# Chunked attention into a two-layer MLP: w_in and w_out loads in halves, the first layer of block 0 in 128-token pieces, s3 on VectorE in the last blocks

## The chip, the cores and the metric

The kernel runs on one core of one Trainium2 chip. The metric is device time in microseconds (us) from one execution; lower is better. A core has five engines that run side by side and wait for each other through semaphores: TensorE (PE in the profile; its weight loads are PEld), VectorE (DVE), ScalarE (ACT), GpSimd (POOL) and SyncE (SP). Work on an engine runs in the order in which it was issued. TensorE writes to PSUM, which has eight banks of 128 x 512 float32; everything else lives in SBUF.

## The reference

```python
# q, k, v: [8 batches, 8 heads, 576, 64], in chunks of 64 tokens, 9 chunks a batch
scores = q_c @ k_c.T / sqrt(64)              # within a chunk only
attn   = softmax(scores)
x      = (attn @ v_c) -> [4608 tokens, 512]  # heads side by side
h      = x @ w_in                            # 512 -> 2048
g      = h * sigmoid(beta * h)
out    = g @ w_out                           # 2048 -> 512
```

Inputs and output are float32; the kernel computes its products in float16 with float32 sums.

## The kernel before

The 4608 tokens are nine blocks j of 512 tokens. For each block there is attention (scores, exponential, product with v, division by the sum), then the first layer L1(j), then the second layer L2(j). The order on every engine is written out by hand: `tc.manual_schedule()` keeps the order of the Python calls, and hooks place pieces of one stage between the matmuls of another. Attention of block j + 1 is placed inside L2(j).

The names that matter here:

- `load_qk`, `load_v`, `load_w_in`, `load_w_out` issue loads on POOL's DMA queue, which convert float32 to float16. w_in comes in four column pieces of 512, w_out in four pieces of four 128-row groups (`kk`, 0 to 15). POOL's transfers use eight completion semaphores in turn.
- `emit_T(b, z, which)` transposes q or k of batch b on VectorE (line 136), one half z at a time.
- `emit_sc(g)` makes scores of four chunks on TensorE (line 168) and their exponentials on ScalarE (line 177). `emit_pv(i, where)` multiplies 128 tokens with v (line 198) and divides on VectorE (lines 210 to 215). `emit_xp(i)` transposes those 128 tokens on TensorE (line 232) and copies them into `xt` (line 235). Blocks 0 and 1 use `emit_xp`; later blocks use a transposing DMA on SP's queue.
- `emit_h(j, m)` is the matmul of L1 for hidden group m (128 of the 2048 hidden columns, line 258); `emit_g(j, m)` is its Silu on ScalarE (line 268). `emit_m` is both. `L1_plain` runs 16 groups in this way for blocks 0 and 1.
- `L2_plain(j)`, block 0 only, is 16 units (four w_out pieces times four 128-token groups), line 510; each token group's last unit copies its bank out, on ScalarE or VectorE in turn (lines 525 and 527), and stores it.
- Blocks 1 to 8 use Strassen-like sums: L2 (`steps_L2`, steps `mm[0]` to `mm[6]`, line 411) needs the sums s1 to s4 of g (`emit_sum`, lines 369 to 375) and t1 to t4 of w_out (`emit_tw`, line 383); from block 2 on L1 (function `L1`) needs sums of x and of w_in (`emit_sw`, lines 280 to 283).
- `scale_w_out` multiplies w_out groups by 1/beta (VectorE line 127, ScalarE line 123), because Silu is applied to beta * h.
- `emit_idle` issues matmuls of zeros; their results aren't used.
- `table(func)` makes ScalarE load the table of a function (line 582).

PSUM is held in three pools: `ps_p` has four one-bank buffers handed out in turn, `ps_s` has two banks (tags sc0 and sc1), and `ps_x` has one buffer of two banks (tag x). A new tile in a buffer waits until the old one has been read. In the last blocks `fill` is a list of sums, which `dve(n)` takes from its head.

s3 is made in four parts. Before the change two of them run on POOL in every block:

```python
tt = (nc.gpsimd if which == 3 and part in (0, 2) else nc.vector).tensor_tensor
```

Of the kernel before, what the change touches and what calls it, by code (L numbers as in the profile page):

```python
# [15 lines left out]
def kernel(  # L16
# [85 lines left out]
                    in_=v[b, h0:h0 + 2].rearrange("s (c p) d -> p (s c) d", p=CH),  # L102
                )

    def load_w_in(g):
        n = DFF // 4
        nc.gpsimd.dma_start(
            out=w_in16[g],
            in_=moe_w_in[:, g * n:(g + 1) * n].rearrange("(k p) f -> p k f", p=128),
        )  # L110

    def load_w_out(g):
        n = NM // 4
        nc.gpsimd.dma_start(
            out=w_out16[:, g * n:(g + 1) * n].rearrange("p m r d -> p m (r d)"),
            in_=moe_w_out[g * n * 256:(g + 1) * n * 256, :].rearrange(
                "(m p r) d -> p m (r d)", p=128, r=2),
        )

    def scale_w_out(g, act=0):  # L120
        for n, kk in enumerate(range(4 * g, 4 * g + 4)):
            if n < act:
                nc.scalar.activation(
                    out=wo(kk), in_=wo(kk), func=ACTF.Copy,
                    scale=binv[:, kk % 2, kk // 2:kk // 2 + 1])
                continue
            nc.vector.tensor_scalar_mul(wo(kk), wo(kk), binv[:, kk % 2, kk // 2:kk // 2 + 1])
# [96 lines left out]
        else:  # L224
            x16_t[i] = xf

    def emit_xp(i):
        xf = x16_t.pop(i)
        j, t0 = i // 4, (i % 4) * 128
        xps = ps_s.tile([128, KDM, 128], FP16, tag=f"sc{i % 2}", name="xps")  # L230
        for kk in range(KDM):
            nc.tensor.transpose(
                out=xps[:, kk, :], in_=xf[:, kk * 128:(kk + 1) * 128], identity=ident
            )
        nc.scalar.copy(out=xt_t[j][:, :, t0:t0 + 128], in_=xps)  # L235

    def emit_idle(n, w=512, d=None):
        if d is None:
# [9 lines left out]
    hps_t = {}  # L248
    w_r = [t.rearrange("p k (m i r) -> p k m r i", r=2, i=128) for t in w_in16]

    def emit_h(j, m, c0=0, c1=BLK):
        if m == 0 and c0 == 0 and j == 0:
            gt_t[j] = gt_p.tile([128, KFF, BLK], FP16, tag="gt", name="gt")
        if c0 == 0:
            hps_t[j, m] = ps_p.tile([128, BLK], FP32, tag="p", name="hps")
        for n in range(KDM):
            e, z = n // 2, n % 2
            nc.tensor.matmul(  # L258
                out=hps_t[j, m][:, c0:c1],
                lhsT=w_r[m // 4][:, 2 * z + e, m // 2 % 2, m % 2, :],  # L260
                rhs=xt_t[j][:, n, c0:c1],
                start=(n == 0),
                stop=(n == KDM - 1),
            )

    def emit_g(j, m):
        hps = hps_t.pop((j, m))
        nc.scalar.activation(  # L268
            out=gt_t[j][:, m, :], in_=hps, func=ACTF.Silu,
            scale=beta2[:, m % 2, m // 2:m // 2 + 1],  # L270
        )
# [89 lines left out]
    def emit_sum(j, which, part):  # L361
        if j not in s_t:
            s_t[j] = [s_p.tile([128, NM, HT], FP16, tag=f"s{i}", name=f"s{i}") for i in range(4)]
        s1, s2, s3, s4 = s_t[j]
        g = gt_t[j]
        lo, hi = slice(2 * part, 2 * part + 2), slice(NM + 2 * part, NM + 2 * part + 2)
        tt = (nc.gpsimd if which == 3 and part in (0, 2) else nc.vector).tensor_tensor
        if which == 1:
            tt(out=s1[:, lo], in0=g[:, lo, dn], in1=g[:, hi, dn], op=ALU.add)  # L369
        elif which == 2:  # L370
            tt(out=s2[:, lo], in0=s1[:, lo], in1=g[:, lo, up], op=ALU.subtract)  # L371
        elif which == 3:
            tt(out=s3[:, lo], in0=g[:, lo, up], in1=g[:, lo, dn], op=ALU.subtract)  # L373
        else:
            tt(out=s4[:, lo], in0=g[:, hi, up], in1=s2[:, lo], op=ALU.subtract)
# [130 lines left out]
    def L2_plain(j):  # L506
        ops = [ps_p.tile([128, DM], FP32, tag="p", name="ops") for _ in range(4)]

        def part(kk, t):
            nc.tensor.matmul(  # L510
                out=ops[t],
                lhsT=gt_t[j][:, kk, t * 128:(t + 1) * 128],
                rhs=wo(kk),
                start=(kk == 0),
                stop=(kk == KFF - 1),
            )

        def unit(g, t):
            for kk in range(4 * g, 4 * g + 4):
                part(kk, t)  # L520
            if g < 3:
                return
            osb = osb_p.tile([128, DM], FP32, tag="osb", name="osb")
            if t % 2:
                nc.vector.tensor_copy(out=osb, in_=ops[t])
            else:
                nc.scalar.copy(out=osb, in_=ops[t])
            r0 = j * BLK + t * 128
            nc.sync.dma_start(out=out[r0:r0 + 128, :], in_=osb)

        return [lambda g=g, t=t: unit(g, t) for g in range(4) for t in range(4)]

    fill = []

# [2 lines left out]
            if fill:  # L537
                fill.pop(0)()

    def L1_plain(j, hooks, nh):  # L540
        if j:
            gt_t[j] = gt_p.tile([128, KFF, BLK], FP16, tag="gt", name="gt")
        for m in range(nh):
            emit_h(j, m, 0, HT)
            hooks.get(-1 - m, lambda: None)()
        for m in range(nh):
            emit_h(j, m, HT, BLK)
            emit_g(j, m)
        for m in range(nh, KFF):
            hooks.get(m, lambda: None)()  # L550
            emit_m(j, m)
            if j and m == 8:
                for p in (0, 2):
                    emit_sum(j, 3, p)
        if j:
            for p in range(4):
                fill.extend([lambda w=w, p=p: emit_sum(j, w, p) for w in (1, 2)])
            hooks.get(KFF, lambda: None)()

    def L1(j, hooks={}, first=None):  # L560
        gt_t[j] = gt_p.tile([128, KFF, BLK], FP16, tag="gt", name="gt")

        def sp(m):
            def f():
                hooks.get(m, lambda: None)()
                emit_m(j, m)
            return f

        if first:
            first()  # L570
        unit(j, 0, [sp(8), sp(9), sp(10)])
        unit(j, 1, [sp(11), sp(12), sp(13)])
        for p in (0, 2):
            emit_sum(j, 3, p)
        for p in (0, 2, 1, 3):
            fill.extend([lambda w=w, p=p: emit_sum(j, w, p) for w in (1, 2)])
        sp(14)()
        sp(15)()
        hooks.get(KFF, lambda: None)()

    def table(func):
        nc.scalar.activation(out=warm2, in_=warm, func=func, scale=1.0)  # L582

    with tc.manual_schedule():
# [11 lines left out]
            nc.vector.memset(t[:, :, :, D:D + 1], 1.0)  # L596
        load_v(0)
        make_identity(nc, ident)
        for g in range(4):
            load_w_in(g)  # L600
        load_w_out(0)
        load_w_out(1)
        load_qk(1)
        load_w_out(2)
        load_v(1)
        load_w_out(3)
        load_qk(2)

        emit_idle(4)
        for f in T_items(0):  # L610
# [13 lines left out]
        emit_sc(1, where="p")  # L624
        emit_idle(3)
        emit_pv(0, xbar=False)
        emit_pv(1, where="p", xbar=False)
        d = emit_idle(4, 256)
        emit_xp(0)
        emit_pv(2, xbar=False)  # L630
        emit_idle(2, d=d)
        emit_xp(1)
        emit_pv(3, where="p", xbar=False)
        emit_idle(3, d=d)

        L1_plain(0, {-2: lambda: emit_xp(2), -3: lambda: emit_xp(3)}, 4)
        emit_sw()
        scale_w_out(0)
        scale_w_out(1)
        emit_tw(1)  # L640
        T1 = T_items(1)
        T1[0]()
        T1[1]()
        T1[2]()
        T1[3]()
        scale_w_out(2, act=2)
        table(ACTF.Exp)
        load_v(2)
        load_qk(3)
        hooks = {  # L650
            8: lambda: [emit_sc(2, "x"), emit_sc(3)],
            10: lambda: [emit_pv(4, xbar=False), emit_pv(5, "s", xbar=False), scale_w_out(3, act=2)],
            12: lambda: [emit_pv(6, xbar=False), emit_xp(4), emit_xp(5)],
            14: lambda: [emit_pv(7, xbar=False), emit_xp(6)],
        }
        for kk, f in enumerate(L2_plain(0)):
            hooks.get(kk, lambda: None)()
# [17 lines left out]
        for j in range(1, NB):  # L675
            na = j + 1
            late = j == 1
            if late:
                L1_plain(1, {
                    -1: lambda: [emit_xp(7), table(ACTF.Silu)], 3: lambda: emit_tw(3), 4: lambda: T(2), 5: lambda: T(2),  # L680
                    6: lambda: emit_tw(2), 7: lambda: T(2), 9: lambda: T(2),
                    10: lambda: emit_tw(4), 14: lambda: T(3), 15: lambda: T(3),
                    11: lambda: [loads(1), loads_v(1)],
                    KFF: lambda: [table(ACTF.Exp), emit_sc(4, "x"), emit_sc(5)],
                }, 3)
            else:
                L1(j, {8: lambda: loads(j), 10: lambda: T(j + 2), 11: lambda: loads_v(j),
                       13: lambda: T(j + 2), 14: lambda: T(j + 2) if j + 2 < B else dve(2),
                       15: lambda: dve(2) if j + 2 >= B else None})

            def pv(n, where):
                if na < NB:
# [80 lines left out]
```

## Time and profile before

| what | value |
|---|---|
| median of 8 runs | 278.48 us (277.59 to 280.51) |
| the profiled execution, its time | 279.58 us |
| its span, first to last instruction | 277.8 us |
| TensorE busy | 263.4 us, 95% of the span |
| VectorE busy | 218.2 us, 79% |
| ScalarE busy | 163.5 us, 59% |
| POOL busy | 102.4 us, 37% |
| first matmul of L1(0), first of L2(0), first of L1(1) | 18.42, 33.37, 50.43 us |
| granted TensorE clock | full over the whole span |

The page lists one execution: busy time of each engine, the span in 40 slices, DMA queues, the chain that ended last, and groups of instructions by line. A row of the timeline gives the start in us, the duration in us, the engine, the line, the operation, what it writes and reads, the shape and how many instructions the row merges; a note in brackets gives how long the engine had been idle and what released it. Waits of an engine are inferred from semaphore events. A time "from start to start" between two instructions of one engine is often shorter than their durations, since they are pipelined.

### The profile page before, as it was taken

The page shows a single profiled execution, that of the slowest core. Times are in us where ns is not written, and L with a number is a line of the kernel's source. Part 1 is how long each engine was busy: PE and PEld are TensorE (multiplying, and loading weights), DVE is VectorE, ACT ScalarE, POOL GpSimd, SP SyncE. Part 2 cuts the span into 40 slices and gives each one's busy share as a digit, 9 for nine tenths or more (in the row PEclk, how much of TensorE's full clock was granted, in tenths as well). Part 3 has the DMA queues.
Part 4 walks back from the last instruction along what each step waited for, and adds up shares of the span by engine and source line. Part 5 has one row for each costly group of instructions (what it writes and reads, how often), then busy time and mean ns, then how long its engine had stood idle before and what let it go on. Part 6 is the DMA issues. An engine that isn't in the chain of part 4 may idle for free.

```text
span 277.8 us, 8206 instructions
## 1 busy us (share of the span) xinstructions
PE 263.4 (95%) x3513; PEld 188.5 (68%) x3513; DVE 218.2 (79%) x425; ACT 163.5 (59%) x276; POOL 102.4 (37%) x108
## 2 busy tenths in 40 slices
PE   2689999999999999999999999999999999999995
PEld 0355454647776688668866886688767866787684
DVE  2772655879588998899889988997689768996874
ACT  2149746788066845783578457845783478216820
POOL 8742252190108720862087205620351035013500
PEclk9999999999999999999999999999999999999999
DMA  6999999999877924892389243924202320232013
GB/s 102 173 207 211 211 182 208 217 238 187 67 134 144 168 46 115 163 166 50 112 155 171 45 117 82 80 46 114 76 2 57 99 76 0 57 100 76 2 38 114
DMA packets 69588, 31.99 MB, mean 115 GB/s; under 512 B 53680, under 2 KB 63920, under 8 KB 69552
## 3 DMA queue, kind: packets, MB, share of 16 engines
q0 software_dynamic: 44960, 18.35, 54.8%
q1 hardware_dynamic: 24448, 12.99, 17.7%
q8 instruction: 27, 0.44, 0.6%
q10 hardware_dynamic: 144, 0.13, 0.1%
q14 instruction: 9, 0.07, 0.1%
HBM read 36.71 MB, written 9.44 MB: 166 GB/s over the span
## 4 chain that ended last, share of the span: by engine, by line
PE 75%; DVE 13%; DMA 6%; issue 2%; POOL 2%; ACT 1%; DVEq 0%; ACTq 0%; POOLq 0%
PE hps L258 24%; PE oA L411 15%; PE wA L311 8%; PE wX L311 6%; PE ops L510 5%; PE oD L411 5%; PE oC L411 3%; PE oB L411 3%; DMA vb<-in_v_dram 3%; DMA xt<-x 3%; DVE x L215 3%; DVE s L369 2%; DVE s L371 2%; PE scx L168 1%; PE sc L168 1%
## 5 line engine op out<-in xcount | busy, mean ns | idle before, releaser
L258 PE MATMUL hps<-xt,wi 128*128 128x512 f16 (+1 forms) x380 | 85.2, 363 | 0.3 <-ACT xt L235 0.2
L268 ACT ACTIVATE gt<-hps,beta 128x512 f16<-128x512 f32 x88 | 57.4, 681 | 20.4 <-PE hps L258 20.3
L258 PEld LDWEIGHTS <-wi 128*128 128x128 f16 x380 | 37.0, 98 | 29.0 <-issue 0.7
L411 PEld LDWEIGHTS <-s 128*128 128x128 f16 x496 | 47.4, 98 | 7.0 <-issue 0.7
L411 PE MATMUL oA<-tw,s 128*128 128x256 f16 x368 | 44.4, 273 | 0.4 <-issue 0.4
L411 PEld LDWEIGHTS <-gt 128*128 128x128 f16 x384 | 36.2, 98 | 6.6
L422 ACT COPY u<-oA 128x512 f32<-128x512 f32 x24 | 14.0, 585 | 44.2 <-PE oA L411 44.2
L99 POOL DMA_DIRECT2D vb<-in_v_dram x32 | 27.4, 874 | 9.2 <-DMA wi<-in_moe_w_in_dram 5.4
L319 DVE COPY u<-wA 128x512 f32<-128x512 f32 x42 | 28.6, 681 | 2.5 <-PE wA L311 2.5
L342 POOL TENSOR_TENSOR t<-u,w 128x512 f32<-128x512 f32 x14 | 17.8, 1273 | 33.1 <-DVE u L319 33.1
L311 PEld LDWEIGHTS <-sw 128*128 128x128 f16 x224 | 21.9, 98 | 9.5 <-issue 1.0
L480 POOL TENSOR_TENSOR o<-t,o 128x512 f32<-128x512 f32 x7 | 8.9, 1271 | 52.4 <-ACT o L477 43.6
L449 POOL TENSOR_TENSOR w<-u,u 128x512 f32<-128x512 f32 x7 | 9.8, 1407 | 44.2 <-ACT u L422 22.8
L136 DVE STREAM_TRANSPOSE qT<-qu 128x576 f32<-128x576 f32 x16 | 20.0, 1251 | 5.0 <-DMA qu<-in_q_dram 5.0
L373 POOL TENSOR_TENSOR s<-gt 128x512 f16<-128x512 f16 x16 | 20.3, 1285 | 9.5 <-ACT gt L268 9.5
L136 DVE STREAM_TRANSPOSE kT<-ku 128x576 f32<-128x576 f32 x16 | 19.9, 1245 | 3.9 <-DMA ku<-in_k_dram 3.9
L369 DVE TENSOR_TENSOR s<-gt 128x512 f16<-128x512 f16 x32 | 20.6, 645 | 0.0
L311 PEld LDWEIGHTS <-wi 128*128 128x128 f16 x168 | 16.4, 98 | 4.9
L371 DVE TENSOR_TENSOR s<-s,gt 128x512 f16<-128x512 f16 x32 | 18.1, 567 | 1.1
L322 ACT ACTIVATE gt<-c,beta 128x512 f16<-128x512 f32 x28 | 18.6, 715 | 0.3
L168 PEld LDWEIGHTS <-kT 32*64 32x64 f16 x1152 | 11.3, 106 | 10.3 <-DVE kT L136 6.5
L582 ACT ACT_TABLE_LOAD x14 | 18.0, 1283 | 0.2
(87 smaller groups left out, 402.6 us busy)
## 6 DMA issues: line engine op xcount, KB each, us to landing
out_dram<-osb SPq DMA_DIRECT2D x21, 256.0 KB, 3.0
vb<-in_v_dram POOLq DMA_DIRECT2D x32, 144.0 KB, 7.8
qu<-in_q_dram POOLq DMA_DIRECT2D x7, 576.0 KB, 7.5
ku<-in_k_dram POOLq DMA_DIRECT2D x7, 576.0 KB, 9.6
out_dram<-o SPq DMA_DIRECT2D x14, 256.0 KB, 2.2
wi<-in_moe_w_in_dram POOLq DMA_DIRECT2D x4, 512.0 KB, 11.9
w_out<-in_moe_w_out_dram POOLq DMA_DIRECT2D x4, 512.0 KB, 16.2
qu<-in_q_dram POOLq DMA_DIRECT2D x2, 288.0 KB, 5.5
```

Of the source, the lines that this page charges most:

```text
L99: nc.gpsimd.dma_start(out=t[64 * hp:64 * hp + 64, 2 * z:2 * z + 2, :, 0:D].rearrange("p s c d -> p (s c) d"), in_=v[b, h0:h0 + 2].rearrang ...
L136: nc.vector.transpose(out=dst[b][:, z].rearrange("p t r e -> p (t r e)").bitcast(FP32).rearrange("p (t r) -> p r t", r=RUN), in_=src[b][:, ...
L258: nc.tensor.matmul(out=hps_t[j, m][:, c0:c1], lhsT=w_r[m // 4][:, 2 * z + e, m // 2 % 2, m % 2, :], rhs=xt_t[j][:, n, c0:c1], start=(n == ...
L268: nc.scalar.activation(out=gt_t[j][:, m, :], in_=hps, func=ACTF.Silu, scale=beta2[:, m % 2, m // 2:m // 2 + 1],)
L311: nc.tensor.matmul(out=bank[b][:, i, :], lhsT=a[:, kk, q, i, :], rhs=rhs[:, kk, :], start=(first and i == 0 and kk == 0), stop=(kk == 1), ...
L319: nc.vector.tensor_copy(out=sb[nm], in_=bank[b])
L322: nc.scalar.activation(out=gt_t[j][:, m, cols], in_=src, func=ACTF.Silu, scale=beta2[:, m % 2, m // 2:m // 2 + 1],)
L369: tt(out=s1[:, lo], in0=g[:, lo, dn], in1=g[:, hi, dn], op=ALU.add)
L371: tt(out=s2[:, lo], in0=s1[:, lo], in1=g[:, lo, up], op=ALU.subtract)
L373: tt(out=s3[:, lo], in0=g[:, lo, up], in1=g[:, lo, dn], op=ALU.subtract)
L411: nc.tensor.matmul(out=bank[name][:, i, :], lhsT=a[:, kk, i * 128:(i + 1) * 128], rhs=b[:, kk, :], start=(first and i == 0 and n == 0), st ...
L582: nc.scalar.activation(out=warm2, in_=warm, func=func, scale=1.0)
```

## The change

It has several parts.

1. The first w_in piece is loaded as two transfers: contraction groups 0 and 2, then 1 and 3. The last w_out piece is loaded as two transfers of two groups each. Batch 1's q and k are loaded in halves z.
2. The first four hidden groups of L1(0) are computed in 128-token pieces (`L1_first`): piece 0 and piece 1 first with half of the contraction, then with the other half; then pieces 2 and 3. The transposes of pieces 1 to 3 and one PV stand between them. Groups 4 to 7 use the banks of `ps_s` and `ps_x` instead of `ps_p`. Piece 3 is copied by VectorE. The last three matmuls of zeros ahead of L1(0) are gone.
3. `L2_plain(0)` has 20 units: the last w_out piece is two pairs of groups. The PVs and transposes of block 1 are spread over more hooks, all PVs on `ps_x`; the last transposes, `emit_xp(7)`, and the load of the Silu table come before its last two units. Batch 1's transposes on VectorE come before `scale_w_out` of the third piece and before `emit_tw(1)`.
4. `L1_plain(1)` computes all 16 groups at 512 columns.
5. For j = 6, 7 and 8 all four parts of s3 are on VectorE, each queued behind the s1 and s2 of the same part.

```diff
-    def load_w_in(g):
+    def load_w_in(g, ks=slice(0, KDM)):
...
-            out=w_in16[g],
+            out=w_in16[g][:, ks],
...
-    def load_w_out(g):
+    def load_w_out(m0, n=2):
...
-    def emit_xp(i):
+    def emit_xp(i, where="s", eng=None):
...
-        xps = ps_s.tile([128, KDM, 128], FP16, tag=f"sc{i % 2}", name="xps")
+        pool, tag = {"s": (ps_s, f"sc{i % 2}"), "p": (ps_p, "p"), "x": (ps_x, "x")}[where]
+        xps = pool.tile([128, KDM, 128], FP16, tag=tag, name="xps")
...
-        nc.scalar.copy(out=xt_t[j][:, :, t0:t0 + 128], in_=xps)
+        if eng:
+            eng.tensor_copy(out=xt_t[j][:, :, t0:t0 + 128], in_=xps)
+        else:
+            nc.scalar.copy(out=xt_t[j][:, :, t0:t0 + 128], in_=xps)
...
-        tt = (nc.gpsimd if which == 3 and part in (0, 2) else nc.vector).tensor_tensor
+        pool = which == 3 and part in (0, 2) and j + 2 < B
+        tt = (nc.gpsimd if pool else nc.vector).tensor_tensor
...
-        return [lambda g=g, t=t: unit(g, t) for g in range(4) for t in range(4)]
+        return [lambda a=a, b=b, t=t: unit(range(a, b), t)
+                for a, b in ((0, 4), (4, 8), (8, 12), (12, 14), (14, 16)) for t in range(4)]
...
+    def L1_first():
+        gt_t[0] = gt_p.tile([128, KFF, BLK], FP16, tag="gt", name="gt")
+
+        def part(t, ns, m_last=False):
+            for m in range(4):
+                emit_h(0, m, t * 128, (t + 1) * 128, ns)
+                if m_last:
+                    emit_g(0, m)
+
+        part(0, (0, 1))
+        emit_xp(1)
+        emit_pv(3, where="s", xbar=False)
+        part(1, (0, 1))
+        part(0, (2, 3))
+        emit_xp(2, "x")
+        part(1, (2, 3))
+        emit_xp(3, eng=nc.vector)
+        table(ACTF.Silu)
+        part(2, range(KDM))
+        part(3, range(KDM), True)
+        for m in range(4, 6):
+            hps_t[0, m] = ps_s.tile([128, BLK], FP32, tag=f"sc{m % 2}", name="hps")
+        hx = ps_x.tile([128, 2, BLK], FP32, tag="x", name="hx")
+        hps_t[0, 6], hps_t[0, 7] = hx[:, 0], hx[:, 1]
+        for m in range(4, KFF):
+            emit_m(0, m)
...
-        for p in (0, 2):
-            emit_sum(j, 3, p)
+        if j + 2 < B:
+            for p in (0, 2):
+                emit_sum(j, 3, p)
...
-        for g in range(4):
+        load_w_in(0, slice(0, KDM, 2))
+        load_w_in(0, slice(1, KDM, 2))
+        for g in range(1, 4):
             load_w_in(g)
         load_w_out(0)
-        load_w_out(1)
-        load_qk(1)
         load_w_out(2)
+        load_qk(1, split=True)
+        load_w_out(4)
         load_v(1)
-        load_w_out(3)
+        load_w_out(6, 1)
+        load_w_out(7, 1)
...
-        emit_pv(1, where="p", xbar=False)
+        emit_pv(1, where="s", xbar=False)
         d = emit_idle(4, 256)
-        emit_xp(0)
+        emit_xp(0, "p")
         emit_pv(2, xbar=False)
         emit_idle(2, d=d)
-        emit_xp(1)
-        emit_pv(3, where="p", xbar=False)
-        emit_idle(3, d=d)
-
-        L1_plain(0, {-2: lambda: emit_xp(2), -3: lambda: emit_xp(3)}, 4)
+
+        L1_first()
         emit_sw()
-        scale_w_out(0)
-        scale_w_out(1)
+        scale_w_out(range(0, 4))
+        scale_w_out(range(4, 8))
+        for f in T_items(1):
+            f()
+        scale_w_out(range(8, 12), act=2)
         emit_tw(1)
...
-            10: lambda: [emit_pv(4, xbar=False), emit_pv(5, "s", xbar=False), scale_w_out(3, act=2)],
-            12: lambda: [emit_pv(6, xbar=False), emit_xp(4), emit_xp(5)],
-            14: lambda: [emit_pv(7, xbar=False), emit_xp(6)],
+            11: lambda: [emit_pv(4, xbar=False), scale_w_out((12, 13), act=1)],
+            12: lambda: [emit_pv(5, xbar=False), emit_xp(4)],
+            14: lambda: [scale_w_out((14, 15), act=1), emit_pv(6, xbar=False), emit_xp(5)],
+            16: lambda: [emit_pv(7, xbar=False), emit_xp(6)],
+            18: lambda: [emit_xp(7), table(ACTF.Silu)],
...
-                    -1: lambda: [emit_xp(7), table(ACTF.Silu)], 3: lambda: emit_tw(3), 4: lambda: T(2), 5: lambda: T(2),
+                    3: lambda: emit_tw(3), 4: lambda: T(2), 5: lambda: T(2),
...
-                       13: lambda: T(j + 2), 14: lambda: T(j + 2) if j + 2 < B else dve(2),
-                       15: lambda: dve(2) if j + 2 >= B else None})
+                       13: lambda: T(j + 2), 14: lambda: T(j + 2) if j + 2 < B else [dve(2), emit_sum(j, 3, 0)],
+                       15: lambda: [dve(2), emit_sum(j, 3, 2)] if j + 2 >= B else None})
```

## The prediction

> **What bounds the kernel now.** I read the page's busy table first, then its chain, then the timeline of all engines over the first 65 us, then each engine's timeline around 192 to 217 us.
>
> ```profile
> PE 263.4 (95%) x3513; PEld 188.5 (68%) x3513; DVE 218.2 (79%) x425; ACT 163.5 (59%) x276; POOL 102.4 (37%) x108
> PE 75%; DVE 13%; DMA 6%; issue 2%; POOL 2%; ACT 1%; DVEq 0%; ACTq 0%; POOLq 0%
> ```
>
> TensorE is the bound, and its work hardly changes. So a gain has to be TensorE idle time, or filler matmuls, that disappear. I subtracted its matmuls' own pace from the spacing of their starts: after 18.4 us only about 4.3 us in all is not paced work. The diff touches two stretches: the start up to the end of L1(1), and the late blocks j = 6, 7, 8.
>
> The start (timeline of all engines):
>
> ```profile
> 16.17 0.40 PE L232 MATMUL xps<-ident,x 128*128 128x128 f16 x4 [0.36 <-DVE x L215]
> 16.61 0.59 ACT L235 COPY xt<-xps 128x512 f16<-128x512 f16 x1 [2.00 <-PE xps L232]
> 17.62 0.58 ACT L235 COPY xt<-xps 128x512 f16<-128x512 f16 x1 [0.42 <-PE xps L232]
> 18.42 1.04 PE L258 MATMUL hps<-xt,wi 128*128 128x256 f16 x8
> 33.37 7.07 PE L510 MATMUL ops<-w_out,gt 128*128 128x512 f16 x32
> 40.37 0.71 PE L168 MATMUL scx<-qT,kT 32*64 32x64 f16 x64
> ```
>
> L1(0) starts at 18.42 because it works on 256 tokens and so needs two copied token pieces; L2(0) starts at 33.37. L1(1) starts at 50.43, the next scores at 64.59, and between them TensorE has no wait above 0.15 us.
>
> Block j = 6 (timelines of VectorE, POOL and the weight loads):
>
> ```profile
> 204.73 0.74 DVE L369 TENSOR_TENSOR s<-gt 128x512 f16<-128x512 f16 x1
> 205.50 1.26 DVE L371 TENSOR_TENSOR s<-s,gt 128x512 f16<-128x512 f16 x1
> 206.69 1.37 DVE L369 TENSOR_TENSOR s<-gt 128x512 f16<-128x512 f16 x1
> 208.10 0.42 DVE L371 TENSOR_TENSOR s<-s,gt 128x512 f16<-128x512 f16 x1
> 209.11 0.20 DVE L213 RECIPROCAL rd<-x 128x8 f32<-128x8 f32 x1
> ...
> 205.14 2.63 POOL L373 TENSOR_TENSOR s<-gt 128x512 f16<-128x512 f16 x2
> ...
> 210.64 0.10 PEld L198 LDWEIGHTS <-et 64*64 64x64 f16 x1 [0.28 <-DVE x L215]
> 211.19 0.20 PEld L198 LDWEIGHTS <-et 64*64 64x64 f16 x15 [0.45 <-DVE x L215]
> ```
>
> While POOL makes two parts of s3, VectorE sums of the same shape take 1.26 and 1.37 us; alone they take 0.42. VectorE thus reaches the softmax division (line 213) at 209.11, and TensorE loses 0.36 and 0.55 us waiting for banks. Block 7 shows the same, 28.6 us later. Block 8 has no such division and no TensorE gap.
>
> **What the Trainium skill says.** "SBUF — State Buffer", Who interferes with whom: a VectorE instruction with two SBUF inputs contends with a GpSimd instruction that reads SBUF. The 1.26 and 1.37 against 0.42 agree. "TensorE: Matmul & The Clock Gate", Back-to-back issue gap: sustained 128-column matmuls with their weight loads run at about 81 ns. The trace differs: the four transposes of 128 columns, each with a load, that begin at 19.29 start 56 ns apart, and there one w_in load follows another after 55 ns. I take 56 and keep 81 as a bound. "ScalarE: Activation LUTs", What ACT_TABLE_LOAD costs: 1283 ns; the trace has 1.28 us. "DMA: Bandwidth & Descriptors", Anatomy of one DMA: about 2 us fixed for each transfer. In the trace queued transfers mostly hide that.
>
> **The change, part by part.**
>
> *w_in in halves.* The first w_in piece has landed by 17.19 (a POOL issue that waited for it starts then), and L1(0) waits for token pieces. Its cover is the copy that ends at 17.20. Moreover the program lets the second matmul wait for both halves. Gain 0. If the extra transfer costs time, the cover is gone: 0.3 us at most is exposed.
>
> *L1(0) in 128-token pieces.* It now needs one copy: start 17.20 + 0.04 = 17.24 instead of 18.42; the three filler matmuls go. But pieces 1 to 3 and PV(3) now lie inside. Steps: 8 matmuls x 0.056 to 17.69; transposes of piece 1, 0.22; its ACT copy runs 18.12 to 18.70. PV(3) now uses banks sc0 and sc1, and sc1 holds those transposes: a new wait, 17.95 to 18.74, with all of L1(0) queued behind it. PV(3) to 19.0; 8 + 8 matmuls 0.90, piece 2 0.22, 8 matmuls 0.45, piece 3 0.22: 20.79. Piece 2's copy ends at 20.91: wait 0.16. Then 32 x 0.056 = 1.8: 22.75. Piece 3's copy on VectorE (0.4 to 0.7 us) is done by 21.7 and hidden; cover gone, it costs its excess. Table load 20.91 to 22.2, hidden by those 32 matmuls. Blocks 4 to 7 go to four other banks, so no Silu holds them. 12 blocks x 0.863: L1(0) ends at 33.10. **Gain 0.27.** At 81 ns it is a loss of 1.3.
>
> *L2(0) in 20 units.* Before 17.06 us (33.37 to 50.43). Now: 64 matmuls x 0.2157 = 13.80; scores 1.21; four PV at 0.25 and four transpose groups at 0.23 (one came out of L1(1)); five changes of kind at 0.09. That is about 17.38, plus one wait: PV(5) now needs the single x bank of PV(4), whose division ends 1.3 us after PV(4)'s start, while 1.2 us of work lies between: 0.11. Sum 17.49. **Loss 0.43.** The other PVs have 1.4 us of cover.
>
> *w_out, batch 1, and their queues.* POOL issues four more transfers (w_in one, w_out one, q and k one each), and each POOL transfer waits for the landing of the eighth before it, so the order stands. q and k of batch 1 came at 32.5 and 35.3; transposes of 1.25 us end by 36.6, scores at 40.1. w_out piece 2 came at 37.9, its scaling is done by 39.4, and it is needed at 41.3; t1, now behind the transposes and that scaling, is needed only in L1(1). The last piece came at 44.07. Its halves are needed at 45.8 and 48.6, ScalarE or VectorE scaling 0.35 to 0.72 before. Cost 0 while every extra transfer costs under 0.75 us. The q loads in halves at the start landed 1.68 us apart, whole ones 2.8: 0.28 each is the nearest row. Below 0: none, nothing waited.
>
> *L1(1).* Full 512-column blocks from the start, xp(7) and the Silu table moved ahead of the last two units. Start 50.59 + 0.03. The copy of the third L2(0) output now stands on ScalarE behind the table load: 50.60 + 1.28 + 0.12 + 0.58 = 52.6, and block 2 needs that bank at 52.35: wait 0.28. 13.80 + 0.28 + 0.10 for the change of kind puts the scores at 64.80 against 64.59. **So the whole start loses 0.2.** Later layers have gaps of their own, which may swallow it.
>
> *s3 on VectorE for j = 6, 7, 8.* POOL loses two 1.3 us instructions a block, VectorE gains two of 0.42 (0.34 from start to start). Block 6, from 205.50: seven sums x 0.34 to 0.45 end at about 208.1 instead of 209.1. The division then waits for PV itself, which ends near 208.28: 0.83 earlier. Its 2.0 us end at 210.30, just as TensorE arrives at 210.2. The gap of 0.91 shrinks to about 0.03: **gain 0.88.** Next late: mm4 waits 0.24 for the last s2, held by POOL's w1; that moves along unchanged. Block 7 likewise 0.88, block 8 0. Sum 1.76; bounds 0.8 (another VectorE wait takes half) and 1.9.
>
> **Sum.** -1.76 + 0.2 = -1.56 us. On its own 279.58 (span 277.8 and 1.8 around it) that is 278.0, or -0.56%. That execution was among the slower: the median is 278.48, so I forecast 276.9. About 0.5% is what a measurement of this kernel can tell from no change.
>
> **The rivals.**
> - *The pieces pay by the load* (81 ns, or half of the late gain lost): +1.6 or +0.9 us on the forecast: 278.5 or 277.8, no difference. For: the skill's figure, longer runs than the trace shows. Against: 55 and 56 ns in the trace.
> - *Split transfers, slower.* If each extra transfer really adds 2 us on a saturated queue (DMA slices at 9 of 10 up to 70 us), the last w_out half lands at 44.07 + 4 x 2 = 52.1, is scaled at 52.8, and L2(0), which needs it at 48.6, waits 4.2: 276.9 + 4.2 = 281.1. It decides from about 0.75 us a transfer and makes the kernel slower by 0.5% from 1.7. For: the skill's fixed cost, 7.35 - 5.67 = 1.68 for half a load. Against: 128-byte v loads of 144 KB land under 1 us apart, so completions overlap.
> - *The start gains after all* (later gaps swallow the 0.2, and the new waits at sc1 and the output bank fall away): 1.1 better: 275.8.
>
> **How the numbers follow.** The forecast 0.42 and the better start 0.08 make faster 0.50. No difference gets 0.37: the pieces' rival 0.27, and 0.10 of forecasts that fall short by 0.2 us. Slower gets 0.13: split transfers 0.08 and their like (instruction fetches, banks) 0.05. Range 275.6 to 279.2: the better start with 0.2 for spread below, the 81 ns case with 0.7 above; the slow case is left out. For the forecast alone it is 276.2 to 277.7.
>
> **What would show it.** Right: L1(0)'s first matmul near 17.2, a wait near 18 on the ACT copy, L2(0) at 33.1, scores after L1(1) near 64.8; in blocks 6 and 7 no sum above 0.8 us ahead of PV, and no TensorE wait at the second PV. Wrong: 128-column matmuls 80 ns apart; a w_out load that TensorE or its scaling waits for; the division still at 209; a gap of 0.5 us or more elsewhere in block 6.

## The result, and the profile after

| | before | after |
|---|---|---|
| median, measured together | 279.01 us (277.59 to 280.51, 32 runs) | 281.71 us (280.47 to 283.53, 11 runs) |
| ratio to before | | 1.0106, 95% interval 1.0085 to 1.0126 |
| the profiled execution, and its span | 279.58, 277.8 us | 281.53, 279.7 us |
| first matmul of L1(0), L2(0), L1(1), L1(2) | 18.42, 33.37, 50.43, 81.23 us | 18.18, 35.40, 53.08, 85.22 us |
| first matmul of L1(6), and from there to the end | 193.1, 84.7 us | 196.6, 83.1 us |

The changed kernel is slower by about 1%, where 0.6% faster was forecast. The last two rows tell where. At L1(2) the changed kernel is 4.0 us behind; until L1(6) it makes up 0.5, and in the last blocks 1.6 of the 1.76 that were forecast.

The profiled pair is 1.95 us apart, the medians 2.7. Of the 11 executions, six took 280.5 to 281.7 us. In the other five TensorE's mean granted clock was only 0.988 to 0.994, and they took 282.0 to 283.5. Ratios here and below leave out the executions in a slow state of the chip and aren't quotients of the medians shown.

The page of the changed kernel: busy time, the queue that carries instructions (packets, MB, share of 16 engines), and the chain.

```profile
PE 264.7 (95%) x3530; PEld 188.6 (67%) x3530; DVE 216.3 (77%) x430; ACT 163.1 (58%) x276; POOL 95.5 (34%) x106
q8 instruction: 27, 0.44, 0.6%
PE 84%; DMA 5%; ACT 3%; DVE 3%; issue 2%; POOL 2%; DVEq 0%; ACTq 0%; POOLq 0%
```

TensorE has 1.3 us more busy time and 17 more matmuls, 34 instructions with their loads. That count will matter. The chain of waits now runs 84% over TensorE, and ScalarE's share rose from 1% to 3%: TensorE waits for it somewhere.

**The start** (timeline of all engines of the changed kernel):

```profile
16.86 0.61 PE L232 MATMUL xps<-ident,x 128*128 128x128 f16 x4
17.50 0.58 ACT L238 COPY xt<-xps 128x512 f16<-128x512 f16 x1 [2.62 <-PE xps L232]
18.18 0.61 PE L259 MATMUL hps<-xt,wi 128*128 128x128 f16 x8
19.69 0.29 PE L197 MATMUL xp<-vb,et 64*64 64x65 f16 x12 [0.53 <-ACT xt L238]
```

The transposes come 0.7 us later than before (16.86 against 16.17), so the one copied piece is ready at 18.08. The second half of w_in lands at 18.15. L1(0) starts at 18.18, not at 17.24. Some 0.6 us of this is the last v piece of batch 0, which landed at 15.45 instead of 14.85. Another 0.3 is TensorE's own pace, as the matmuls of zeros show (timeline of TensorE, changed kernel, then kernel before):

```profile
13.55 1.46 PE L244 MATMUL idle<-zero 128*128 128x512 f16 x3
```

```profile
13.00 0.82 PE L241 MATMUL idle<-zero 128*128 128x512 f16 x3
```

The same three take 1.46 us instead of 0.82: half pace. It lasted until 17.7 us in this execution, in the kernel before until 11.6. The full clock that the pages and the table of the kernel before give for these first stretches is only the absence of a record: the traces' clock records begin at 17.66 and 11.63. In the profile with group 7 moved (below) v landed as late, TensorE ran at full pace, and L1(0) started at 17.84.

The 0.53 at 19.69 is the forecast wait of PV(3) for the copy out of sc1. The next two views show the first surprise (timeline of TensorE, then of ScalarE):

```profile
25.58 1.03 PE L259 MATMUL hx<-xt,wi 128*128 128x512 f16 x4
27.63 1.02 PE L259 MATMUL hx<-xt,wi 128*128 128x512 f16 x4 [1.02 <-ACT gt L270]
```

```profile
26.86 0.72 ACT L270 ACTIVATE gt<-hx,beta 128x512 f16<-128x512 f32 x1
28.69 0.69 ACT L270 ACTIVATE gt<-hx,beta 128x512 f16<-128x512 f32 x1 [1.11 <-PE hx L259]
```

Hidden group 6 fills the first bank of the tile hx. Group 7 goes into the second bank, yet it starts at 27.63, just after the Silu that reads the first (26.86 + 0.72). From the last matmul of group 6 to the first of group 7 it is 1.40 us where the pace is 0.22, so 1.18 us are lost.

**The second surprise** is in L2(1) (timeline of TensorE, changed kernel, then kernel before):

```profile
72.16 0.27 PE L197 MATMUL xp<-vb,et 64*64 64x65 f16 x12
74.21 0.22 PE L197 MATMUL xp<-vb,et 64*64 64x65 f16 x4 [1.78 <-issue]
74.37 0.83 PE L414 MATMUL oA<-tw,s 128*128 128x256 f16 x6
```

```profile
69.77 1.70 PE L411 MATMUL oA<-tw,s 128*128 128x256 f16 x14
71.91 0.39 PE L411 MATMUL oA<-tw,s 128*128 128x256 f16 x2 [0.44 <-issue]
```

The 16 matmuls of one PV stop after twelve, for 1.97 us, and "issue" says that the profile names no engine and no load that they wait for. In the kernel before, the same sort of gap (0.72 us from start to start, 0.61 beyond the pace) splits the 16 matmuls of a step of L2(1), 36 TensorE instructions further on. Each gap follows a packet on the instruction queue: the packet starts at 69.56 and TensorE goes on at 71.91; in the changed kernel at 71.86 and 74.21, 2.35 us later both times. I read this as TensorE waiting for its own instructions. 27 packets of 16 KB for some 7,060 TensorE instructions make one packet for about 260.

A count supports the reading. In ten profiles of this document TensorE has pauses of this sort before 77 us. Counted in matmuls and weight loads from the start of the kernel, they come after number 446, 1214, 1724 or 1726, or 1980, whatever stands there: a whole number of blocks of 256 apart, to within two.

**Block 6** (timeline of VectorE, then of the weight loads, changed kernel):

```profile
209.03 0.42 DVE L374 TENSOR_TENSOR s<-s,gt 128x512 f16<-128x512 f16 x1
209.37 0.42 DVE L376 TENSOR_TENSOR s<-gt 128x512 f16<-128x512 f16 x1
211.82 0.21 DVE L212 RECIPROCAL rd<-x 128x8 f32<-128x8 f32 x1 [0.24 <-PE x L197]
```

```profile
211.45 0.33 PEld L197 LDWEIGHTS <-et 64*64 64x64 f16 x32 [0.21 <-issue]
213.68 0.43 PEld L197 LDWEIGHTS <-et 64*64 64x64 f16 x30 [0.21 <-DVE rd L209]
```

No sum ahead of PV takes 1.3 us any more, the division starts as soon as PV has its first bank, and the second PV waits 0.21 instead of two gaps of 0.36 and 0.55. This part did what was forecast.

### The profile page after: what moved, and what is told of

The parts are those of the page before. It is cut to its first block, busy times and chain, and to the rows that moved or that the text cites. A ratio compares the mean times of both kernels' runs of the same rounds, so it can differ in the third digit from the quotient of the medians.

```text
span 279.7 us, 8242 instructions
## 1 busy us (share of the span) xinstructions
PE 264.7 (95%) x3530; PEld 188.6 (67%) x3530; DVE 216.3 (77%) x430; ACT 163.1 (58%) x276; POOL 95.5 (34%) x106
## 4 chain that ended last, share of the span: by engine, by line
PE 84%; DMA 5%; ACT 3%; DVE 3%; issue 2%; POOL 2%; DVEq 0%; ACTq 0%; POOLq 0%
PE hps L259 24%; PE oA L414 18%; PE wA L313 9%; PE wX L313 6%; PE oB L414 5%; PE oD L414 5%; PE ops L513 4%; PE oC L414 4%; DMA vb<-in_v_dram 3%; PE x L197 2%; PE scx L167 2%; PE sc L167 2%; DMA xt<-x 1%; ACT gt L270 1%; PE xp L197 1%
## 5 line engine op out<-in xcount | busy, mean ns | idle before, releaser
L259 PE MATMUL hps<-xt,wi 128*128 128x512 f16 (+1 forms) x392 | 83.5, 353 | 0.1
L270 ACT ACTIVATE gt<-hps,beta 128x512 f16<-128x512 f32 x86 | 56.4, 681 | 20.6 <-PE hps L259 20.6
L372 DVE TENSOR_TENSOR s<-gt 128x512 f16<-128x512 f16 x32 | 17.8, 555 | 0.5 <-ACT gt L270 0.5
L313 PE MATMUL wA<-xs,sw 128*128 128x256 f16 x112 | 16.8, 272 | 0.5 <-DVE u L321 0.5
L374 DVE TENSOR_TENSOR s<-s,gt 128x512 f16<-128x512 f16 x32 | 15.6, 488 | 1.1
```

Of the source, the lines that this page charges most:

```text
L259: nc.tensor.matmul(out=hps_t[j, m][:, c0:c1], lhsT=w_r[m // 4][:, 2 * z + e, m // 2 % 2, m % 2, :], rhs=xt_t[j][:, n, c0:c1], start=(n == ...
L270: nc.scalar.activation(out=gt_t[j][:, m, :], in_=hps, func=ACTF.Silu, scale=beta2[:, m % 2, m // 2:m // 2 + 1],)
L313: nc.tensor.matmul(out=bank[b][:, i, :], lhsT=a[:, kk, q, i, :], rhs=rhs[:, kk, :], start=(first and i == 0 and kk == 0), stop=(kk == 1), ...
```

## The experiments

The theory after this reading: three things cost time, the pair of banks in hx, the fetch of instructions behind the loads, and a later start of L1(0). The rival: the start is slow in itself, and these gaps only lie where it is seen. Every ratio is to the kernel before, measured on the same chip.

| run | median us (runs) | ratio, 95% interval |
|---|---|---|
| after | 281.71 (11) | 1.0106, 1.0085 to 1.0126 |
| before + s3 edit | 277.03 (6) | 0.9930, 0.9903 to 0.9956 |
| after, group 7 in its own bank | 281.31 (16) | 1.0062, 1.0037 to 1.0087 |
| after, v load moved | 280.21 (13) | 1.0066, 1.0039 to 1.0093 |
| after, both | 278.61 (22) | 0.9986, 0.9975 to 0.9996 |
| before + 34 instructions | 283.42 (6) | 1.0171, 1.0133 to 1.0210 |
| before + 34, v load moved | 280.72 (6) | 1.0065, 1.0045 to 1.0085 |
| before + s3 edit, v load moved | 278.10 (12) | 0.9962, 0.9946 to 0.9978 |
| after + 222 instructions | 279.86 (22) | 1.0026, 1.0016 to 1.0037 |
| before + s3 edit + 222 instructions | 282.24 (6) | 1.0090, 1.0060 to 1.0119 |
| after, group 7 and 222 instructions | 279.07 (16) | 1.0006, 0.9992 to 1.0020 |
| after, first w_in piece whole | 280.83 (6) | 1.0060, 1.0036 to 1.0084 |
| after, both fixes, all loads whole | 278.40 (12) | 0.9972, 0.9954 to 0.9990 |

**The s3 edit alone.** The kernel before with part 5 of the change only.

```diff
-        tt = (nc.gpsimd if which == 3 and part in (0, 2) else nc.vector).tensor_tensor
+        pool = which == 3 and part in (0, 2) and j + 2 < B
+        tt = (nc.gpsimd if pool else nc.vector).tensor_tensor
...
```

> The kernel before with only the s3 edit: for j = 6, 7, 8 all parts of s3 on VectorE, queued as in the changed kernel. Theory (the late part works as forecast and the loss is all in the start): no TensorE gap at the second PV of blocks 6 and 7, 1.5 to 1.8 us less than before, ratio near 0.994. Rival (the late gain in the changed kernel is only time that its later start had lost before): less than 0.8 us, ratio 0.997 or more.

Measured: 277.03 us, 1.8 less than the 278.86 of the kernel before beside it. This version is faster than both kernels. Its timeline of VectorE in block 6:

```profile
204.82 0.43 DVE L372 TENSOR_TENSOR s<-s,gt 128x512 f16<-128x512 f16 x1
205.16 0.42 DVE L374 TENSOR_TENSOR s<-gt 128x512 f16<-128x512 f16 x1
207.62 0.21 DVE L213 RECIPROCAL rd<-x 128x8 f32<-128x8 f32 x1 [0.24 <-PE x L198]
```

From L1(6) to the end it takes 83.1 us, as the changed kernel does, against 84.7 before. So the late part is sound, and all of the loss lies ahead of block 6.

**Group 7 in a bank of its own.** The rest of the changed kernel stays.

```diff
-        hps_t[0, 6], hps_t[0, 7] = hx[:, 0], hx[:, 1]
+        hps_t[0, 6] = hx[:, 0]
```

> The changed kernel, but hidden group 7 of L1(0) gets a ps_p bank of its own instead of the second half of the two-bank x tile. Theory (the two halves are one tile, so group 7 waits for group 6's Silu, which stands behind six others): the wait of about 1.0 to 1.2 us near 26 us is gone, L2(0) starts near 34.2 instead of 35.4, and the time falls by 1.2 us (0.4%) against the changed kernel, unless the later instruction fetch gives it back. Rival (the 128-column pieces or the table load are what is late, and group 7 only shows it): the wait moves to group 8 or later and L2(0) still starts near 35.4.

The wait is gone: L1(0) takes 16.02 us instead of 17.22, and L2(0) starts at 33.86. The median is only 0.4 us lower, but the ratio fell by 0.44%, 1.2 us. The median misleads because the executions fall into two sorts: the eight with a mean granted clock of 0.997 or more have a median of 279.7 us, the other eight 281.9. For the changed kernel the first sort (six of 11) has 281.2, so where the clock held, the gain was about 1.6.

The fetch gap grew to 2.14 us, and in the profiled execution something else follows it. In the table by windows, the third figure from the end of a row is the granted TensorE clock; the first pairs are busy times of TensorE, its loads, VectorE, ScalarE and POOL:

```profile
70.00:72.80 2.80, 0.90 (x34) 0.58 (x32) 0.90 (x2) 0.36 (x1) 0.00 (x0) 1.00 1.12 74
72.80:76.00 3.20, 3.15 (x24) 2.45 (x24) 1.12 (x4) 0.42 (x1) 0.00 (x0) 0.71 0.38 77
76.00:78.00 2.00, 2.00 (x13) 1.52 (x12) 0.00 (x0) 0.16 (x1) 1.26 (x1) 0.61 0.09 17
78.00:80.00 2.00, 2.00 (x49) 1.61 (x47) 1.28 (x4) 0.00 (x0) 0.00 (x0) 1.00 0.00 0
```

From 74.2 to 77.5 us matmuls of 256 columns start 213 ns apart instead of 109: TensorE runs at half pace, which costs another 1.7 us. This case comes back at the end.

**The v load moved.** The v load of batch 3 is issued after L2(1) instead of in L1(1); the rest of the changed kernel stays.

```diff
-                    11: lambda: [loads(1), loads_v(1)],
+                    11: lambda: loads(1),
...
             mm[6]()
+            if late:
+                loads_v(1)
```

> The changed kernel, but the v load of batch 3 is issued after L2(1) instead of in the middle of L1(1); nothing else. Theory (TensorE's stall of 1.97 us at 72.2 is an instruction fetch that queues behind loads on the full DMA engines): with no v packets there the stall shrinks to under 0.5 us and the time falls by 1.4 to 2.0 us. Rival A (the stall is the PV waiting for a bank or for v): it stays at about 2 us. Rival B (the fetch has a fixed delay that load doesn't change): it stays at about 2 us.

The boundary lies at the same instruction, but the gap is gone (timeline of TensorE of this run; the sixteen are whole):

```profile
73.96 0.32 PE L197 MATMUL x<-vb,et 64*64 64x65 f16 x16
74.10 0.30 PE L197 MATMUL xp<-vb,et 64*64 64x65 f16 x16
74.33 1.92 PE L414 MATMUL oA<-tw,s 128*128 128x256 f16 x16
```

The median falls by 1.5 us. Smaller gaps of 0.5 us appear at 107 and 116 us; there TensorE waits for VectorE, and the run with the s3 edit and the moved load shows why. (This profiled execution ran at half pace from 17.4 to 24.2 us, so how long its L1(0) took isn't read.)

**34 instructions added to the kernel before.** 17 matmuls of 16 columns on zeros near 3 us, while TensorE waits for the first q: the change's own count, and nothing else of it.

```diff
-        emit_idle(4)
+        d0 = emit_idle(4)
+        emit_idle(17, 16, d=d0)
```

> The kernel before plus 17 matmuls of zeros of 16 columns near 3 us, where TensorE waits for the first q and k; they shift all later TensorE instructions by 34 places, as the changed kernel does, and cost no time there. Theory (where the boundary between fetched instruction blocks falls decides the stall): the gap near 71 us grows from 0.6 to about 2 us and moves from the second L2 matmuls into the PV ahead of them; time up by 1.0 to 1.5 us, ratio near 1.004. Rival (the stall depends on what the changed kernel loads or waits for): gap 0.6 us as before, ratio 1.000.

It costs 4.6 us, more than the whole change does and three times what was expected. The 0.6 us gap moves back into the PV and grows (timeline of TensorE):

```profile
70.15 0.29 PE L198 MATMUL xp<-vb,et 64*64 64x65 f16 x13
72.77 0.22 PE L198 MATMUL xp<-vb,et 64*64 64x65 f16 x3 [2.33 <-issue]
```

Further gaps of 0.83 and 1.18 us came up in a PV at 17.4 and in scores at 220 us.

**The same with the v load moved.**

> The kernel before with 34 more TensorE instructions near 3 us (17 matmuls of 16 columns on zeros), and with the v load of batch 3 issued after L2(1). The 34 alone gave 283.4 us, with a 2.5 us gap at 70 us. Theory (the stall needs both the fetch and the load): the 2.5 us gap goes, what is left of the 4.5 us is the other gaps (0.8 us at 17.4, 1.2 us at 220): 280.4 to 281.2 us. Rival (where the fetched block ends decides alone): the gap stays above 1.5 us and the time at 283.

280.72 us: the 2.5 us gap is gone, the other ones stay. When the instruction packet starts, counted in us from the first matmul of mm0(1) (step mm[0] of L2(1)), shows why:

```
                          v load in flight   v load moved
before                    3.8                0.7  (with the s3 edit)
before + 34 instructions  3.9                0.2
after                     3.4                0.2
after, group 7 moved      3.6                0.4
```

With the load out of the way the packet starts about 3 us earlier, and TensorE never waits for it. Counted from the moment when TensorE passes the previous such place, 256 instructions ahead, it starts 0.9 to 1.3 us later with the load moved and 3.8 to 4.6 us later with the load in flight. The Trainium skill ("DMA: Bandwidth & Descriptors", Queues, rings and completion order) says that an engine takes turns between its queues, a packet at a time. No run here shows the turns or how long one is; what makes the delay as long as 3 us isn't settled.

A load in flight isn't needed for a pause, though. The one in the scores stayed (timeline of TensorE of this run):

```profile
216.87 0.72 PE L168 MATMUL sc<-qT,kT 32*64 32x64 f16 x62
218.93 0.22 PE L168 MATMUL sc<-qT,kT 32*64 32x64 f16 x2 [1.34 <-issue]
```

The DMA engines were less than half busy there, and the packet started 0.6 us after the previous place. But the 256 instructions between were short and took TensorE only 1.4 us.

**The s3 edit and the moved v load on the kernel before.**

> The kernel before with the s3 edit alone, and with the v load of batch 3 issued after L2(1) instead of in L1(1). Theory (the 0.6 us stall of TensorE near 71 us is an instruction fetch that queues behind that load's 128-byte packets): the stall at 71 us goes, a smaller one (0.5 us at most) may appear near 107 us; about 276.4 us against 277.0 of the s3 edit alone, ratio to the kernel before 0.989 to 0.993. Rival (the stall is the fetch alone, whatever else is loading): the gap at 71 us stays 0.6 us and the time stays at 277.0, or rises by what the late load costs in L1(2).

The theory's gap at 71 us went, and L1(2) started 0.6 us earlier, but the time rose by about 1 us to 278.10. The lead is lost by L1(4), which starts at 137.7 against 136.8. Gaps of 0.41 at 102.7 and 0.63 at 111 us came with the late load. They aren't fetches: TensorE waits for VectorE (timelines of POOL, VectorE and TensorE of this run, and the same VectorE sum in the run with the s3 edit alone):

```profile
83.62 3.43 POOL L99 DMA_DIRECT2D vb<-in_v_dram  x4
100.93 1.52 POOL L450 TENSOR_TENSOR w<-u,u 128x512 f32<-128x512 f32 x1 [4.09 <-DVE s L370]
101.24 1.49 DVE L370 TENSOR_TENSOR s<-gt 128x512 f16<-128x512 f16 x1
103.24 1.26 PE L412 MATMUL oA<-tw,s 128*128 128x256 f16 x10 [0.25 <-DVE s L372]
```

```profile
100.64 0.42 DVE L370 TENSOR_TENSOR s<-gt 128x512 f16<-128x512 f16 x1
```

The moved load takes 3.4 us of POOL's time to issue. POOL, busy without a break from there on, came to its parts of s3 0.8 us later (94.30 against 93.53), and two VectorE sums now ran beside POOL's work: 1.26 and 1.49 us instead of 0.42. So the expectation for the time was wrong. The collision with the fetch went, and the one that the s3 edit removes from the last blocks came up in block 2. The rival's clause on what the late load costs is what happened.

**Both missed costs removed from the changed kernel.**

> The changed kernel with hidden group 7 of L1(0) in a bank of its own and with the v load of batch 3 issued after L2(1). Theory (these two are the missed costs): both gaps (1.2 us at 26, 2 us at 72) are gone, 0.5 us may come near 107: 281.5 - 1.2 - 2.0 + 0.5 = about 278.8 us, that is within 0.3% of the kernel before, and still 1.5 to 2 us above the s3 edit alone, from the late start of L1(0), its longer run and L2(0). Rival (the start costs nothing but these two): 277.0, level with the s3 edit alone. Rival (time won early is lost again before L1(3)): above 280.

278.61 us, as the theory had it (timeline of TensorE: no wait at hx):

```profile
24.70 1.03 PE L259 MATMUL hx<-xt,wi 128*128 128x512 f16 x4
25.56 7.93 PE L259 MATMUL hps<-xt,wi 128*128 128x512 f16 x36
```

In the medians each alone gave 0.4 and 1.5 us, and both together 3.1. That looks as if the second cost ate the first. The clock says otherwise: none of the 22 executions here has a mean clock under 0.998, against 5 of 11 of the changed kernel and 8 of 16 with group 7 moved. By the executions at 0.997 or more the two alone give about 1.6 and 1.4 us (281.2 to 279.7 and 279.8), and both 2.6 (278.6), so they nearly add up.

**The boundary moved instead of the load.** 111 matmuls of 16 columns on zeros near 3 us; with the change's own 34 instructions that is 256 more ahead than in the kernel before.

```diff
-        emit_idle(4)
+        d0 = emit_idle(4)
+        emit_idle(111, 16, d=d0)
```

> The changed kernel with 111 more matmuls of 16 columns on zeros near 3 us, while TensorE waits for the first q. With the change's own 34 that makes 256 TensorE instructions more than the kernel before has ahead of mm2(1), one whole fetched block, so that the boundary falls where the kernel before has it. Theory (which instruction the boundary falls on sets the stall): the 2 us gap moves from PV at 72 us to mm2 near 73 us and shrinks to 0.5 to 0.8 us; 281.7 - 1.3 = 280.4 us. Rival (the later time of the fetch, or the moved loads, set it): 1.5 us or more at either place, 281.7 us or above.

```profile
71.82 1.47 PE L414 MATMUL oA<-tw,s 128*128 128x256 f16 x12
73.44 0.49 PE L414 MATMUL oA<-tw,s 128*128 128x256 f16 x3 [0.15 <-issue]
```

The gap is back in the step in which the kernel before has it, and is 0.3 us beyond the pace. 222 *more* instructions made the kernel 1.85 us faster, and the page counts 28 packets instead of 27. This is the clearest proof that the place of the boundary, not the work added, cost the time.

**The same 222 on the kernel before with the s3 edit.**

> The kernel before with the s3 edit and the same 111 matmuls, 222 instructions: the boundary that stalled TensorE 0.6 us at 71 us now falls 34 instructions later. Theory: the fetch is then asked for at about 70.5 to 71.5 us, when the v load of batch 3 (landed by 71.7) is nearly through, and the gap shrinks to 0 to 0.4 us: 276.4 to 277.0 us, if no other boundary finds a load; it would be the fastest version. Rival (any shift of the boundaries costs, as the 34 did): a gap of 1 us or more somewhere and 278 us or above.

The rival was right: 282.24 us. The gap at 71 us is gone, but another boundary now falls into a PV of L2(0) (timeline of TensorE):

```profile
44.86 0.20 PE L198 MATMUL xp<-vb,et 64*64 64x65 f16 x3
47.95 0.31 PE L198 MATMUL xp<-vb,et 64*64 64x65 f16 x13 [2.89 <-issue]
48.19 3.38 PE L511 MATMUL ops<-w_out,gt 128*128 128x512 f16 x8
```

Again the packet starts (45.5) 2.45 us before TensorE goes on. The last w_out piece had landed at 44.8, and q and k of batch 2 were on their way, in packets of 2,304 bytes where those of v have 128; so it needn't be small packets. Of the eight matmuls after it the last five start 0.43 us apart instead of 0.216: half pace again, until about 52 us.

**Group 7 and the boundary together.**

> The changed kernel with group 7 of L1(0) in a bank of its own and the 111 matmuls near 3 us that put the fetched block's boundary where the kernel before has it; the v load of batch 3 stays in L1(1). Theory (the two missed costs add up, and what is left of the new start costs about 0.7 us against the old one): the 1.2 us wait goes, the fetch gap stays near 0.3 us; 279.9 - 1.2 = 278.7 us at most, 277.8 us at least, ratio 0.995 to 0.999. Rival (the 1.2 us is swallowed again, as in the run where group 7 alone was moved): 279.5 us, with a fetch gap of 1 us or more.

279.07 us, where the kernel before took 278.58 beside it. The ratio is only 0.2% better than the boundary alone and misses the range that was expected. Its profiled execution ran at half clock from 15 to 25 us, so its stages aren't read.

**The first w_in piece whole.**

```diff
-        load_w_in(0, slice(0, KDM, 2))
-        load_w_in(0, slice(1, KDM, 2))
-        for g in range(1, 4):
+        for g in range(4):
```

> The changed kernel with the first w_in piece loaded whole again. Theory (the first half overtakes the last v piece of batch 0): that v piece lands near 14.7 us instead of 15.4, the first transposes start at 16.1 instead of 16.8, the whole w_in piece lands at 17 to 17.9, L1(0) starts at 17.5 to 18.0 instead of 17.8 to 18.2: a gain of 0.2 to 0.6 us, 281.2 us. Rival (the landing of v differs by chance): v lands near 15.4 as before and L1(0) starts at 18.1 or later; no gain, or a loss of up to 0.5 us since the second half is waited for longer.

```profile
16.66 0.59 ACT L238 COPY xt<-xps 128x512 f16<-128x512 f16 x1 [1.78 <-PE xps L232]
17.50 0.45 PEld L259 LDWEIGHTS <-wi 128*128 128x128 f16 x8 [0.58 <-DMA wi<-in_moe_w_in_dram]
```

L1(0) starts at 17.51, now held by the landing of the whole piece (17.46) and not by the copy, which ends at 17.25. 280.83 us, 0.9 less, or 0.4 less than the 281.2 of the changed kernel's executions at a mean clock of 0.997 or more. The last v piece landed at 14.90; with the halves it landed at 14.9 to 15.45 in five profiles. The theory of overtaking fits most of them, not all.

**All loads whole, with both fixes.** Besides the above, the last w_out piece and q and k of batch 1 are one transfer each again.

> The changed kernel with group 7 in a bank of its own, the v load of batch 3 after L2(1), and the first w_in piece, the last w_out piece and q and k of batch 1 whole again. The same with the halves gave 278.6 us. Theory (only the first w_in piece's halves cost, by the late last v piece and the second half): L1(0) starts near 17.5, the waits for w_out stay zero since 2 tokens' worth of units cover it: 278.0 to 278.6 us. Rival (each of the four extra transfers costs): 277.5 us or less, with L2(0) earlier by 0.5 us or more. Rival (the halves are needed): a wait for w_out between 45 and 49 us, 279 us or more.

278.40 against 278.61 with the halves, intervals that overlap. TensorE never waits for w_out in either. So the split transfers neither help nor hurt to a degree that can be told here, and whether the 0.9 of the run before is the halves' own stays open.

## Why the prediction was wrong

The forecast had a gain of 1.56 us; the profiled pair shows a loss of 1.95, which is 3.5 apart. (The medians lose 0.75 more; the executions at a lower mean clock account for it at least in part, since the others have a median of 281.2.) Step by step:

| step of the prediction | forecast | measured |
|---|---|---|
| L1(0) begins | 17.24 | 18.18 (17.3 to 18.2 in five profiles with halves) |
| L1(0) lasts | 15.86 | 17.22; 16.02 with group 7 moved |
| L2(0) lasts | 17.49 | 17.68 |
| scores after L1(1) begins | 14.18 | 14.14 |
| L2(1): gap of TensorE | not in the sum | 1.97 instead of 0.61: 1.36 |
| late blocks | -1.76 | -1.6 |

- **The step that failed first** is "Blocks 4 to 7 go to four other banks, so no Silu holds them." The banks are four, but two of them are one tile, and the write of group 7 waited for the read of group 6. It cost 1.18 us in the profile. In the ratios its removal gave 0.2% with the boundary moved as well, 0.4% alone and 0.8% with the load moved as well, that is 0.6 to 2.2 us; half pace in some executions is in these.
- **The term that wasn't there** is "So the whole start loses 0.2." It counted added matmuls at their own pace and nothing for the instructions as such. The 0.61 us gap on "issue" at 71 us stood in the trace of before and was left among "gaps of their own", which might swallow a loss; it was a gap that any added instruction moves. In medians its removal gave 1.5 (load moved) to 1.85 us (boundary moved), and 1.3 to 1.4 by the executions at a mean clock of 0.997 or more, where the profile has 1.36. The prediction did name both causes, "instruction fetches, banks", but with a share of 0.05 and no cost.
- **The start of L1(0)** was too early by 0.9 in this execution, of which about 0.6 is the late v piece and 0.3 half pace, both in part chance. In the three profiles with halves that ran at full pace there it was too early by 0.1 to 0.6. The cover of the w_in halves was named, "the copy that ends at 17.20", with 0.3 at most exposed; both the copy and the second half came near 18.1.
- **Right:** the pace of 56 ns (L1(0) without the hx wait: 16.02 against 15.86), the wait of PV(3) behind sc1 (0.74 against 0.79 from start to start), the wait for the third output bank (0.24 against 0.28), no TensorE wait for w_out or batch 1's q and k, so no cost of w_out and batch 1, and s3 (1.8 us in the median of the run with it alone). The wait of PV(5) was 0.32, not 0.11.
- **The rivals:** "Split transfers, slower" had the right sign and about the right time, 281.1, but by luck: its cause, a wait for w_out, didn't come. Nor did the pieces pay by the load.
- **Open:** with both missed costs away, the changed kernel takes 278.6 to 279.1 us against 277.0 of the s3 edit alone, 0.6 to 0.8% of ratio. Against the s3 edit with the v load moved as well (278.1) it is only 0.5, and the intervals touch. The profiles show 0.85 us at L1(1) (51.02 against 50.17, both with that load moved), but later gaps swallow it: both begin L2(2) at 94.2 and span 276.2. What the new start costs where nothing else interferes thus lies between nothing and 2 us, against the 0.2 of the forecast, and isn't settled closer.

## What to carry to other kernels

Before you price an edit by its matmuls, look for idle time on "issue" and for the instruction packet ahead of it: where loads are in flight or the boundary can fall into very short instructions, adding instructions may cost or gain 2 us or more, and no count of work shows it. Two banks held as one tile were one buffer to the waits here. A load that is moved takes the time of the engine that issues it along, here 3.4 us of POOL. Look at the granted clock of every execution before you trust a median: here it hid most of a gain of some 1.5 us. When a change has independent parts, measure them apart: here one part alone was faster by 0.7%, and the sum was slower by 1.1%.

## What the runs showed of the hardware

- TensorE's instructions came in packets of 16 KB on a DMA queue of their own, one for 256 instructions, as the places of the pauses show. From the start of a late packet until TensorE went on took 2.2 to 2.5 us in ten profiles. In L2(1) the pause was 1.7 to 2.5 us where PV (64 instructions in some 0.45 us) stood at the boundary, and 0.3 to 0.6 where matmuls of 256 columns did.
- A pause can cost twice. After pauses of 2.1 and 3.1 us TensorE ran at half pace, with a granted clock of 0.50 from 74.16 to 77.58 and from 48.45 to 51.86 us, 3.4 us each time. The Trainium skill ("TensorE: Matmul & The Clock Gate", Part 1) tells of half clock after an idle window of about 3.4 us that runs freely; here pauses shorter than that window were enough. They weren't each time: pauses of 1.97 us (changed kernel) and 2.5 us (34 instructions) left the pace whole in their profiles, while with the v load moved half pace set in at 17.4 us with no pause longer than 1.2 us in the 3.4 us before. With the 34 added instructions, three of six executions had a mean granted clock of 0.992 to 0.994 and took 284.2 to 284.9 us; the three at 0.999 or above took 282.4 to 282.7.
